# RMSNorm attention followed by a hard-swish MLP: moving the norms, joining the transposes, and issuing stores and output transposes later

## The chip, the cores and the metric

The kernel runs on one core of a Trainium2 chip. The metric is the device time of that core in microseconds (us). A run counts as slow when it is more than 1.5% above the fastest run of the same kernel; the kernel before was run again on the same chip beside every experiment. The kernel after was not: it is compared with an experiment through the ratios to the kernel before.

Names of the engines: PE is the matrix engine (PEld its weight loads), DVE the vector engine, ACT the scalar engine, POOL the general engine, SP the engine that here does nothing but issue DMA. Each executes its own list of instructions in order. An instruction that waits holds up everything behind it on its engine, related or not.

## The reference

Eight batches of twelve heads, 448 tokens, head size 64; then an MLP over the 3,584 tokens.

```python
def rmsnorm(x, g):
    rms = np.sqrt(np.mean(x * x, axis=-1, keepdims=True) + 1e-06)
    return x / rms * g
q_n, k_n = rmsnorm(q, g_q), rmsnorm(k, g_k)            # q, k, v: (8, 12, 448, 64)
scores = np.matmul(q_n, k_n.transpose(0, 1, 3, 2)) / np.sqrt(64)
attn = softmax(scores)                                 # over the keys
x = np.matmul(attn, v) -> (3584, 768)                  # heads side by side
h = x @ w_in                                           # (3584, 2048)
g = h * np.clip(h + 3.0, 0.0, 6.0) / 6.0
return g @ w_out                                       # (3584, 768), float32
```

## The kernel before

The kernel works on 48 pairs of heads, six pairs to a batch. Of a head's 448 tokens, 384 are "main" tokens (three blocks of 128); the remaining 64, the "rest tokens", are collected for all heads of two batches and normed and transposed together.

For a pair P: load q, k, v (SP); square (ACT for the first pairs, later POOL), sum (DVE), Ln and Exp (ACT) give the factor `rs`; POOL scales q and k into bf16 (`qks`) and copies v (`va`); SP issues crossbar transposes of `qks`; DVE multiplies the transposed keys with a mask and the gains (`kp`); PE makes seven score matmuls, ACT their exponentials, PE the products with v; DVE normalises into `xn`; SP transposes `xn` into `xT`. While batch b is in attention, PE also does h of batch b-1 (`h_part`, whose gate `gT` is made by DVE) and y of batch b-2 (`y_part`, copied from PSUM, the memory that PE writes its results to, by DVE into `y_sb` and stored by SP). The lists of SP and POOL stand in the order in which the program emits them. Cuts are marked; a comment starting with "note" is not in the kernel.

```python
def prep_pair(P):                       # note: norm and scaling of a pair in one go
    qk, vf = st.pop(("qk", P)), st.pop(("vf", P))
    sq = sq_pool.tile([128, 4 * NT * D], FP32, name="sq", tag="sq")
    qk_flat = qk[:].rearrange("p a h x -> p (a h x)")
    square(sq[:], qk_flat, P < 3)
    ssq = st_pool.tile([128, 4 * NT], FP32, name="ssq", tag="ssq")
    nc.vector.tensor_reduce(
        out=ssq[:], in_=sq[:].rearrange("p (n d) -> p n d", d=D), axis=AX_X, op=A_ADD)
    rs = rstd_of(ssq[:], 4 * NT)        # note: Ln, then Exp, both on ACT
    # ... cut: rs4 ...
    qks = qks_pool.tile([128, 2, NT, 2, D], BF16, name="qks")
    for i in range(2):
        nc.gpsimd.tensor_tensor(        # note: L162, waits on POOL for rs
            out=qks[:, i].rearrange("p t h d -> p h t d"),
            # ... cut ...
            op=A_MULT)
    # ... cut: POOL copies v into the ring va (L168) ...

def trans_rest(b):                      # note: rest tokens of batches b and b+1
    qks = st.pop(("qkrs", b))
    rT = rst_pool.tile([128, 2, NPAIR, 128], BF16, name="rT")
    nc.sync.dma_start_transpose(
        out=rT[:].rearrange("p a j c -> p (a j) c"), in_=qks[:].rearrange("p a h d -> p (a h d)"))
    for e in range(2):
        part = rT[:, :, :, e * 64:(e + 1) * 64]
        nc.vector.tensor_copy(out=qT_of(b + e)[:, :, SM:S], in_=part[:, 0])
        # ... cut: kbd, the masked rest keys, two multiplies on DVE ...

def trans_pair(P):
    b, j = divmod(P, NPAIR)
    qks = st.pop(("qks", P))
    nc.sync.dma_start_transpose(                                    # note: L237
        out=qT_of(b)[:, j, 0:SM].rearrange("p (t c) -> p t c", t=NT),
        in_=qks[:, 0].rearrange("p t h d -> p (t h d)"))
    kT = kT_pool.tile([128, SM], BF16, name="kT")
    nc.sync.dma_start_transpose(                                    # note: L241
        out=kT[:].rearrange("p (t c) -> p t c", t=NT),
        in_=qks[:, 1].rearrange("p t h d -> p (t h d)"))
    kp = kp_pool.tile([128, 2, SM], BF16, name="kp")
    for a in range(2):
        nc.vector.tensor_scalar_mul(kp[:, a, :], kT[:], gmask[:, a:a + 1])   # note: L246
    st["kp", P] = kp

def xtrans_rest(b, j0):                 # note: rest rows of x, three pairs
    xr = st["xr", b // 2]
    for j in range(j0, j0 + 3):
        nc.sync.dma_start_transpose(out=xT_of(b)[:, j, SM:SM + 128], in_=xr[:, j, :])

def y_part(G, i, nh, part):
    # ... cut: four matmuls per part, four parts ...
    if part == 3:
        y_sb = y_pool.tile([128, HALF], FP32, name="y_sb")
        nc.vector.tensor_copy(out=y_sb[:], in_=y_ps)                # note: L366
        cols = slice(nh * HALF, (nh + 1) * HALF)
        if i < NT:
            rows = out[G * S:G * S + SM, cols].rearrange("(p t) n -> t p n", t=NT)[i]
            nc.sync.dma_start(out=rows, in_=y_sb[:])                # note: L370
        # ... cut: rest rows, two stores (L374) ...

def att_items(P):
    b, j = divmod(P, NPAIR)
    n = P + 1
    items = [(0.0, lambda: load_step(P + 5)), (0.0, lambda: prep_step(P + 3)),
             (0.0, lambda: trans_step(P + 2))]
    sc = [(0.19, lambda u=u: score(n, u)) for u in range(NU)] if n < NP else []
    vs = [(0.3, lambda t=t: av(P, t)) for t in range(NT + 1)]
    items += merge(sc, vs)
    items.append((0.0, lambda: xtrans(P)))
    # ... cut: xtrans_rest after every third pair of odd batches ...
    return items

# ... cut ...
with tc.manual_schedule(engines={mybir.EngineType.SP, mybir.EngineType.Pool}):
    for P in range(5):
        load_step(P)
    for P in range(3):
        prep_step(P)
        if P < 2:
            trans_step(P)
    for u in range(NU):
        score(0, u)
    # ... cut: for each batch, the items of its six pairs merged with h and y items ...
```

## Time and profile before

| | before |
|---|---|
| median of three runs | 625.91 us (623.76 to 630.04) |
| profiled run: span, mean granted clock | 623.8 us, 0.901 |
| first exponential of pair 0, of pair 12, of pair 42 | 30.3, 161.4, 483.8 us |
| time of one batch in steady state (batches 4 to 6) | 64.7, 65.7, 66.1 us |

The "first exponential of pair n" is the (7n+1)th of the 336 score exponentials on ACT in the trace. It is a good clock of progress: batch b runs from the first exponential of pair 6b to that of pair 6b+6. I cut the span at pairs 0, 12 and 42 into start, front (pairs 0 to 11, while the MLP weights are loaded), steady part (pairs 12 to 41) and end.

The first lines of the profile page of the kernel before. Part 1 gives busy us, share of the span and number of instructions; part 2 shows the span in 40 slices, busy share in tenths, with the clock granted to PE; part 4 is the chain of work that ended last.

```profile
span 623.8 us, 9051 instructions
...
PE 461.5 (74%) x3344; PEld 257.1 (41%) x3344; DVE 253.5 (41%) x496; ACT 302.8 (49%) x582; POOL 212.8 (34%) x243
...
PE   0065234676579777969798989596988789789997
...
PEclk9997665799599998979799889898899999797999
...
issue 37%; POOL 24%; PE 16%; DMA 12%; SPq 6%; DVE 3%; POOLq 0%; ACT 0%; ACTq 0%
```

No engine is saturated. PE is the fullest with 74%, and the chain that ended last is made of PE for 16% only: it runs through POOL, DMA and "issue" (time in which an engine waited for nothing that the profile shows). In part 2 the slices of PE from the third to the eleventh (31 to 171 us) are on the whole the emptiest after the first two, and there the clock is lowest. So the kernel is bound by waits. Next, the view of windows for the three sections: us, then the busy time of each engine, PE's clock, DMA share, GB/s.

```profile
core 0: us, PE busy (x) PEld busy (x) DVE busy (x) ACT busy (x) POOL busy (x), PEclk, DMA share, GB/s
30.30:161.40 131.10, 70.60 (x540) 38.90 (x539) 44.89 (x94) 60.81 (x126) 56.21 (x63) 0.78 0.73 141
161.40:483.80 322.40, 268.45 (x1992) 149.04 (x1991) 151.89 (x294) 186.35 (x358) 136.51 (x146) 0.92 0.44 113
483.80:623.80 140.00, 121.87 (x812) 68.81 (x811) 48.95 (x94) 48.03 (x83) 9.23 (x11) 0.95 0.21 57
```

PE is busy for 71 of 131 us in the front, 268 of 322 in the steady part and 122 of 140 at the end. Which waits fill the rest shows the view of waits: what waited, for what, us in total, how many times, the longest.

```profile
POOL qks L162 <- ACT rs L128: 181.2, 44, 18.8
...
DVE kp L246 <- DMA kT<-qks: 130.6, 39, 11.4
PEld L261 <- DVE kp L246: 72.0, 28, 27.0
...
PE s_ps L261 <- DVE kp L246: 34.2, 21, 7.7
```

And the same view for the DMA queue of SP, i.e. what stood between SP and its next issue:

```profile
SPq L370 <- DVE y_sb L366: 127.8, 35, 7.8
...
SPq L374 <- DVE y_sb L366: 15.1, 5, 4.1
```

The waits of DVE, of PE and of SP form a ring. A few lines of the timeline at 212 us (start, duration, engine, line, operation; in brackets how long the engine sat idle before it, and for what) show one turn of it:

```profile
212.08 1.20 SPq L241 DMA_TRANSPOSE kT<-qks  x1
...
214.52 1.41 DVE L246 TENSOR_SCALAR kp<-kT,gmask 128x384 bf16<-128x384 bf16 x2 [2.44 <-DMA kT<-qks]
...
216.55 0.68 DVE L350 SCALAR_TENSOR_TENSOR gT_1502<-t_sb,h_ps 128x512 bf16<-128x512 f32 x1
217.14 0.55 DVE L366 COPY y_sb<-y_ps 128x384 f32<-128x384 f32 x1
217.28 0.81 PE L360 MATMUL y_ps<-w_out_sb,gT_819 128*128 128x384 bf16 x4 [1.16 <-DVE gT_1502 L350]
...
217.72 0.36 SPq L370 DMA_DIRECT2D out_dram<-y_sb  x1
```

SP issues the key transpose at 212.08, right before it is needed. DVE stands at the first instruction in its list that needs it, `kp`, and is idle for 2.44 us. Behind `kp` in DVE's list stand a gate and a y copy whose inputs are from earlier work; they run at 216.55 and 217.14. PE waits for that gate (217.28), which frees the PSUM buffer that h and y take in turn, and the store on SP can only go after the y copy (217.72). Only then does SP come to what stands behind the store: the next loads and transposes. SP waits for DVE; DVE waits for SP's transposes.

### The profile page before, as it was taken

What the parts mean: (1) busy time and instruction counts of PE and PEld (TensorE: products, weight loads), DVE (VectorE), ACT (ScalarE), POOL (GpSimd) and SP (SyncE); (2) the same over time, 40 slices, a digit from 0 to 9 for tenths busy, and PEclk for the clock granted to TensorE, in tenths of its full rate; (3) what the DMA queues carried; (4) which work ended last, traced back from release to release, by engine and by line L of the source; (5) the groups of instructions that cost most, each with busy time, mean ns of one, the idle gap of its engine ahead of it and who ended that gap; (6) DMA issues with size and microseconds to landing.
All of it is one profiled execution on the core that took longest, in us unless ns stands there. A gap on an engine that the chain in (4) does not pass through costs nothing.

```text
span 623.8 us, 9051 instructions
## 1 busy us (share of the span) xinstructions
PE 461.5 (74%) x3344; PEld 257.1 (41%) x3344; DVE 253.5 (41%) x496; ACT 302.8 (49%) x582; POOL 212.8 (34%) x243
## 2 busy tenths in 40 slices
PE   0065234676579777969798989596988789789997
PEld 0033122344145444535354546353544356454554
DVE  1342031264454544436346354353354543233331
ACT  2365223566466564646366655463656556332310
POOL 0745042455656332464135334552344220000000
PEclk9997665799599998979799889898899999797999
DMA  9498665994444245444353538343434332120012
GB/s 211 90 150 183 128 131 107 152 157 103 114 115 134 77 133 123 121 123 111 76 138 86 136 93 184 91 123 81 130 96 117 93 92 56 48 43 27 26 56 72
DMA packets 139660, 67.46 MB, mean 108 GB/s; under 512 B 92768, under 2 KB 138848, under 8 KB 139616
## 3 DMA queue, kind: packets, MB, share of 16 engines
q1 hardware_dynamic: 133184, 59.81, 39.2%
q0 software_dynamic: 2976, 6.29, 6.0%
q10 hardware_dynamic: 3456, 0.79, 0.8%
q8 instruction: 26, 0.43, 0.3%
q14 instruction: 18, 0.15, 0.1%
HBM read 45.61 MB, written 11.01 MB: 91 GB/s over the span
## 4 chain that ended last, share of the span: by engine, by line
issue 37%; POOL 24%; PE 16%; DMA 12%; SPq 6%; DVE 3%; POOLq 0%; ACT 0%; ACTq 0%
POOL sq L135 9%; PE y_ps L360 9%; POOL qks L162 8%; PE h_ps L343 6%; DMA kT<-qks 5%; SPq L332 3%; DMA qkr<-in_k_dram 2%; POOL vbd_89 L194 1%; POOL vbd_92 L194 1%; SPq L237 1%; PE s_ps L261 1%; SPq L325 1%; POOL sqr L135 1%; DMA qk<-in_k_dram 1%; POOL vbd_95 L194 1%
## 5 line engine op out<-in xcount | busy, mean ns | idle before, releaser
L262 ACT ACTIVATE eT<-s_ps,zero_c 128x448 bf16<-128x448 f32 x336 | 203.6, 635 | 158.7 <-PE s_ps L261 157.5
L261 PE MATMUL s_ps<-qT,kp 128*128 128x448 bf16 x288 | 112.3, 407 | 65.1 <-DVE kp L246 34.2
L162 POOL TENSOR_TENSOR qks<-qk,rs 128x384 bf16<-128x384 f32 x96 | 77.8, 832 | 189.7 <-ACT rs L128 181.2
L343 PEld LDWEIGHTS <-w_in_sb 128*128 128x128 bf16 x768 | 75.4, 102 | 109.5 <-issue 57.1
L348 ACT ACTIVATE t_sb<-h_ps,half_c 128x384 f32<-128x384 f32 (+1 forms) x128 | 80.6, 632 | 71.0 <-PE h_ps L343 70.5
L246 DVE TENSOR_SCALAR kp<-kT,gmask 128x384 bf16<-128x384 bf16 x96 | 43.0, 489 | 130.6 <-DMA kT<-qks 130.6
L270 PEld LDWEIGHTS <-eT 128*128 128x128 bf16 x1152 | 69.1, 104 | 58.8 <-DVE xn L289 18.7
L261 PEld LDWEIGHTS <-kp 128*128 128x128 bf16 x288 | 30.2, 107 | 112.4 <-DVE kp L246 72.0
L135 POOL TENSOR_TENSOR sq<-qk 128x768 f32<-128x768 f32 x45 | 66.2, 1471 | 0.2
L156 DVE TENSOR_REDUCE ssq<-sq 128x12 f32<-128x768 f32 x48 | 45.5, 948 | 30.9 <-POOL sq L135 22.8
L366 DVE COPY y_sb<-y_ps 128x384 f32<-128x384 f32 x56 | 30.8, 551 | 20.4 <-PE y_ps L360 20.2
L127 ACT ACTIVATE rs<-ssq,eps_c 128x12 f32<-128x12 f32 x48 | 14.6, 304 | 46.1 <-DVE ssq L156 46.0
L343 PE MATMUL h_ps<-xT_896,w_in_sb 128*128 128x512 bf16 x96 | 28.3, 395 | 8.4 <-DVE y_sb L366 5.0
L343 PE MATMUL h_ps<-xT_380,w_in_sb 128*128 128x384 bf16 x96 | 25.0, 378 | 12.5 <-DMA xT_380<-xn 10.2
L343 PE MATMUL h_ps<-xT_2374,w_in_sb 128*128 128x512 bf16 x96 | 28.2, 402 | 5.3 <-DMA xT_2374<-xr 4.2
L343 PE MATMUL h_ps<-xT_1599,w_in_sb 128*128 128x384 bf16 x96 | 22.3, 340 | 12.6 <-DVE y_sb L366 9.6
L343 PE MATMUL h_ps<-xT_3983,w_in_sb 128*128 128x512 bf16 x96 | 27.8, 397 | 4.3 <-DMA xT_3983<-xr 2.8
L343 PE MATMUL h_ps<-xT_5596,w_in_sb 128*128 128x512 bf16 x96 | 27.2, 406 | 3.1 <-DMA xT_5596<-xr 3.1
L360 PE MATMUL y_ps<-w_out_sb,gT_1502 128*128 128x384 bf16 x128 | 28.2, 343 | 0.3 <-DVE y_sb L366 0.3
L343 PE MATMUL h_ps<-xT_4817,w_in_sb 128*128 128x384 bf16 x96 | 21.9, 337 | 8.7 <-DVE y_sb L366 5.4
L360 PE MATMUL y_ps<-w_out_sb,gT_4720 128*128 128x384 bf16 x128 | 27.3, 338 | 1.1 <-DVE gT_5480 L350 1.0
L343 PE MATMUL h_ps<-xT_3208,w_in_sb 128*128 128x384 bf16 x96 | 22.1, 337 | 7.9 <-DVE y_sb L366 6.6
(81 smaller groups left out, 636.3 us busy)
## 6 DMA issues: line engine op xcount, KB each, us to landing
qk<-in_q_dram SPq DMA_DIRECT2D x48, 192.0 KB, 2.7
qk<-in_k_dram SPq DMA_DIRECT2D x48, 192.0 KB, 2.7
vf<-in_v_dram SPq DMA_DIRECT2D x48, 192.0 KB, 3.3
out_dram<-y_sb SPq DMA_DIRECT2D x48, 192.0 KB, 1.9
w_in_sb<-in_moe_w_in_dram POOLq DMA_DIRECT2D x6, 512.0 KB, 8.3
w_out_sb<-in_moe_w_out_dram POOLq DMA_DIRECT2D x4, 768.0 KB, 7.6
vr<-in_v_dram SPq DMA_DIRECT2D x16, 96.0 KB, 3.4
out_dram<-y_sb SPq DMA_DIRECT2D x16, 96.0 KB, 2.2
```

The lines of the kernel that those rows point to most:

```text
L135: nc.gpsimd.tensor_tensor(out=out, in0=x, in1=x, op=A_MULT)
L156: nc.vector.tensor_reduce(out=ssq[:], in_=sq[:].rearrange("p (n d) -> p n d", d=D), axis=AX_X, op=A_ADD)
L162: nc.gpsimd.tensor_tensor(out=qks[:, i].rearrange("p t h d -> p h t d"), in0=qk[:, i].rearrange("p h (t d) -> p h t d", d=D), in1=rs4[:, i ...
L194: nc.gpsimd.tensor_scalar(vbd[:, :, a * E1:a * E1 + D], vr[:], mask[:, a:a + 1], None, A_MULT)
L246: nc.vector.tensor_scalar_mul(kp[:, a, :], kT[:], gmask[:, a:a + 1])
L261: nc.tensor.matmul(out=ps[:], lhsT=lhsT, rhs=st["qT", b][:, j, :], start=True, stop=True)
L262: nc.scalar.activation(out=st["e", P][:, u, :], in_=ps[:], func=EXP, bias=zero_c[:], scale=1.0)
L270: nc.tensor.matmul(out=dst[:, a * E1:(a + 1) * E1], lhsT=eT[:, u, c0:c0 + 128], rhs=va[:, a, t, :], start=(first and a == 0 and t == 0), s ...
L343: nc.tensor.matmul(out=h_ps[:, 0:n], lhsT=w_in_sb[:, kt, f * 128:(f + 1) * 128], rhs=st["xT", G][:, kt, :], start=(kt == 0), stop=(kt == N ...
L348: nc.scalar.activation(out=t_sb[:, 0:n], in_=h_ps[:, 0:n], func=RELU, bias=half_c[:], scale=1.0 / 6.0)
L360: nc.tensor.matmul(out=y_ps, lhsT=gT[:, f, i * 128:(i + 1) * 128], rhs=w_out_sb[:, f, nh * HALF:(nh + 1) * HALF], start=(f == 0), stop=(f ...
L366: nc.vector.tensor_copy(out=y_sb[:], in_=y_ps)
```

## The change

Its intent, in the words that came with it: norms one pair ahead of the scaling; one crossbar transpose for keys and queries of a pair; stores and output transposes issued later; rest tokens loaded first. In parts:

- **norm**: square, sum, Ln and Exp of pair P+4 are done in the step before the scaling of that pair, so POOL's scaling finds `rs` ready. Loads go to P+6.
- **joined transposes**: one transpose of six blocks of 128x128 (keys, then queries) in place of two of three; one of three for the rest rows of x in place of three of one. It costs a DVE copy of 64 rest columns per pair and one of `xrT` per half.
- **store**: the store of a y group is emitted in the middle of the next group. **late xT**: the transpose of `xn` is emitted near the end of the next pair's step.
- **start**: three pairs loaded before the first norms instead of five, keys before queries, rest loads split over SP and ACT, rest scaling of batch 0 on DVE.

The core of the diff; cuts are pool sizes (`st_pool` 4 to 8, `y_pool` 3 to 4, four `kq` buffers in place of three `kT` and three `qT`), the weight of the value products when lists are merged (0.3 to 0.25), squares on ACT for four pairs instead of three, the split of `prep_rest` alike to that of `prep_pair`, and engine choices of the first loads.

```diff
-    def prep_pair(P):
-        qk, vf = st.pop(("qk", P)), st.pop(("vf", P))
+    def norm_pair(P):
+        qk = st["qk", P]
         sq = sq_pool.tile([128, 4 * NT * D], FP32, name="sq", tag="sq")
 # ... cut ...
-        rs = rstd_of(ssq[:], 4 * NT)
+        st["rs", P] = rstd_of(ssq[:], 4 * NT)
+
+    def prep_pair(P):
+        qk, vf, rs = st.pop(("qk", P)), st.pop(("vf", P)), st.pop(("rs", P))
 # ... cut ...
     def trans_pair(P):
-        b, j = divmod(P, NPAIR)
         qks = st.pop(("qks", P))
+        kq = kq_pool.tile([128, SM + S], BF16, name="kq")
         nc.sync.dma_start_transpose(
-            out=qT_of(b)[:, j, 0:SM].rearrange("p (t c) -> p t c", t=NT),
-            in_=qks[:, 0].rearrange("p t h d -> p (t h d)"))
-        kT = kT_pool.tile([128, SM], BF16, name="kT")
-        nc.sync.dma_start_transpose(
-            out=kT[:].rearrange("p (t c) -> p t c", t=NT),
-            in_=qks[:, 1].rearrange("p t h d -> p (t h d)"))
+            out=kq[:, 0:2 * SM].rearrange("p (t c) -> p t c", c=128),
+            in_=qks[:].rearrange("p a t h d -> p (a t h d)"))
+        st["kq", P] = kq
+
+    def pad_pair(P):
+        b, j = divmod(P, NPAIR)
+        kq = st.pop(("kq", P))
+        e = (b % 2) * 64
+        nc.vector.tensor_copy(out=kq[:, 2 * SM:], in_=st["rT", b // 2][:, 1, j, e:e + 64])
         kp = kp_pool.tile([128, 2, SM], BF16, name="kp")
         for a in range(2):
-            nc.vector.tensor_scalar_mul(kp[:, a, :], kT[:], gmask[:, a:a + 1])
+            nc.vector.tensor_scalar_mul(kp[:, a, :], kq[:, 0:SM], gmask[:, a:a + 1])
+        st["qT", P] = kq[:, SM:]
         st["kp", P] = kp
 # ... cut ...
     def xtrans_rest(b, j0):
         xr = st["xr", b // 2]
-        for j in range(j0, j0 + 3):
-            nc.sync.dma_start_transpose(out=xT_of(b)[:, j, SM:SM + 128], in_=xr[:, j, :])
+        xrT = xr_pool.tile([128, 3, 128], BF16, name="xrT")
+        nc.sync.dma_start_transpose(
+            out=xrT[:], in_=xr[:, j0:j0 + 3, :].rearrange("p j c -> p (j c)"))
+        nc.vector.tensor_copy(out=xT_of(b)[:, j0:j0 + 3, SM:SM + 128], in_=xrT[:])
 # ... cut ...
     def y_part(G, i, nh, part):
+        if part == 2:
+            flush_stores()
 # ... cut ...
+            stores.append(lambda: y_store(G, i, nh, y_sb))
 # ... cut ...
-        items = [(0.0, lambda: load_step(P + 5)), (0.0, lambda: prep_step(P + 3)),
-                 (0.0, lambda: trans_step(P + 2))]
+        items = [(0.0, lambda: load_step(P + 6)), (0.0, lambda: norm_step(P + 4)),
+                 (0.0, lambda: trans_step(P + 2)), (0.0, lambda: prep_step(P + 3))]
 # ... cut ...
-        items.append((0.0, lambda: xtrans(P)))
-        if b % 2 == 1 and j % 3 == 2:
-            items.append((0.0, lambda: xtrans_rest(b, j - 2)))
+        items.insert(len(items) - 6, (0.0, flush_late))
+
+        def done():
+            late.append(lambda: xtrans(P))
+            if b % 2 == 1 and j % 3 == 2:
+                late.append(lambda: xtrans_rest(b, j - 2))
+            if j == NPAIR - 1:
+                flush_late()
+        items.append((0.0, done))
 # ... cut ...
-        for P in range(5):
+        for P in range(3):
             load_step(P)
-        for P in range(3):
+        norm_step(0)
+        norm_step(1)
+        for P in range(2):
             prep_step(P)
-            if P < 2:
-                trans_step(P)
+            trans_step(P)
+            load_step(P + 3)
+            norm_step(P + 2)
+        prep_step(2)
+        load_step(5)
```

## The prediction

> **What bounds the kernel now.** Nothing is saturated: PE is busy 461.5 of 623.8 us, ACT 302.8, DVE 253.5, POOL 212.8 (page, part 1). Warm and fed, PE needs about 440 us (estimate from trace durations: 336 scores at 0.19, 192 groups of seven small value products at 0.45, 768 + 896 MLP matmuls at 0.19 and 0.163 us). The kernel is bound by waits in in-order queues:
> 1. Start: first score at 29.7 us (timeline); the rest tokens' keys are loaded last, issuing them holds ACT until 12.65 us, and the score needs the rest transpose.
> 2. 30 to 161 us (pairs 0 to 11): PE half busy. POOL's scaling waits 181.2 us in all for the ACT root of its own pair (view of waits), so transposes go out late and meet weight loads (one key transpose: issued 61.0, used 73.5 us). DMA is about 75% busy (windows).
> 3. Batches 4 to 6: 65 us each, PE busy 56 (windows). SP waits 127.8 us for y_sb before stores, transposes queued behind; DVE waits 130.6 us for kT before kp, gate and y_sb copies queued behind; PE waits 106 us for kp.
>
> **What the change does.**
> - Norm of pair P+4 ahead of scaling of P+3: POOL no longer waits for reduce, Ln, Exp (4 us per pair); this reaches PE only through the transposes.
> - 48 pair transposes and 16 of the rest of x fewer, 1.2 us of SP issue each: 77 us of SP. Added on DVE: 48 copies of 64 columns, 8 of xrT, about 10 us, which has room.
> - Stores wait for the next y group, xT transposes for the end of the next pair: their data are then ready and block nothing. kp should be ready a step early.
> - Start: three pairs loaded instead of five, keys of the rest second, 2.75 instead of 3.9 MB before the first score; qkrs scaled on DVE.
> - Matmuls, exps and bytes unchanged.
>
> **On the critical path.** Start: -10 us. 30 to 161: -28 (weights took 37 us of 16-engine DMA time, a pair about 4.4, so 100 us is near the floor). Batches 2 and 3: -13. Batches 4 to 6: -5 each of a possible 8, since h still waits at each batch start for the last xT. Batch 7 and end: -4. Sum -70: **555 us, 530 to 590** (8 in 10). Faster by over 2% 0.95, within 2% 0.04, slower 0.01.
>
> The Trainium skill ("TensorE: Matmul & The Clock Gate", the HAM clock gate) says PE falls to half clock after an idle window of about 3.4 us. This trace agrees: scores take 581 ns around the stalls at 75 to 125 us, 349 later. Fewer gaps should raise the mean clock from 0.90 to about 0.94, part of the gain above.
>
> **What would show it.** First score at 19 us. First exp of pair 12 at 120 to 135 us (161 before). POOL's wait for ACT below 40 us, SP's for y_sb below 15, DVE's for pair transposes below 50, PE's for kp below 35. Batches 4 to 6 at 59 us. PE share 80% or more.
>
> **What would make it wrong.** If early DMA is already at its limit, the front yields only the start. If one transpose of six blocks lands much later than the 2.4 us of three, or behind six pairs of loads, kp stays late. If steady waits merely become h waiting for xT (xr now passes through DVE) or PSUM waiting for y_sb, batches stay at 65 us: about 590. If PE takes all the room, 530.

## The result, and the profile after

| | before | after |
|---|---|---|
| median | 625.62 us (four runs) | 532.87 us (526.60 to 535.94, four runs) |
| ratio of fast runs, 95% interval | | 0.8475 (0.8384 to 0.8566) |
| profiled run: span, clock | 623.8 us, 0.901 | 530.6 us, 0.945 |
| start (to the first exponential) | 30.3 us | 24.1 us |
| front, pairs 0 to 11 | 131.1 us | 94.7 us |
| steady part, pairs 12 to 41 | 322.4 us | 290.8 us |
| end, pair 42 on | 140.0 us | 121.0 us |
| batches 4, 5, 6 | 64.7, 65.7, 66.1 us | 57.0, 62.6, 58.0 us |

The ratios are made from fast runs; they are not quite the ratios of the medians quoted. The change is 15% faster, more than predicted, inside the range. The profiled spans differ by 93.2 us: start 6.2, front 36.5, batches 2 and 3 together 12.5, batches 4 to 6 together 18.9, batch 7 and the end 19.1.

The same lines of the page of the kernel after:

```profile
span 530.6 us, 8957 instructions
...
PE 433.2 (82%) x3316; PEld 251.9 (47%) x3344; DVE 262.6 (49%) x546; ACT 299.4 (56%) x583; POOL 210.7 (40%) x244
...
PE   0245559957899987799799988589798999999996
...
PEclk9985768979999999899899999899999999999999
...
PE 45%; DMA 20%; issue 11%; DVE 10%; POOL 8%; SPq 4%; ACT 1%; POOLq 0%; DVEq 0%
```

PE now makes 45% of the chain that ended last, where it made 16%. One trap: the page counts 3,316 matmuls and 3,344 weight loads. 28 records of h matmuls are missing from this trace, 24 in the steady part and 4 at the end; at 0.28 us each (busy time of the recorded ones of that shape over their number, as their records overlap) PE was busy some 8 us longer than the page says, about 441 us. Still 20 us less than before for the same matmuls, because the clock was higher. Idle times of PE below are corrected in this way, for this trace and for the experiments that lack the same 28 records.

The windows of the sections, with the columns of before:

```profile
24.10:118.80 94.70, 62.10 (x490) 35.11 (x488) 45.30 (x97) 59.08 (x126) 60.06 (x66) 0.77 1.04 205
118.80:409.60 290.80, 255.63 (x2018) 149.37 (x2042) 158.08 (x332) 185.27 (x359) 130.90 (x140) 0.98 0.56 128
409.60:530.60 121.00, 114.90 (x807) 67.08 (x811) 47.32 (x95) 46.65 (x81) 6.11 (x8) 1.00 0.20 55
```

The front's DMA share rose from 0.73 to 1.04, which suggests that the front is now held by what it loads; experiment 11 tests it. (The share counts the times of packets, and reaches 1.13 in the first half of this front: 1 is not its ceiling.) In the steady part PE is idle for about 28 us instead of 54, at a clock of 0.98 instead of 0.92. At the end PE is idle for about 5 us instead of 18, and works at full clock, 116 us (corrected) instead of 122.

The waits that answer to those of before:

```profile
DVE kp L250 <- DMA kq<-qks: 82.4, 30, 10.6
POOL va L171 <- PE r_ps L275: 80.4, 17, 7.1
POOL va L171 <- PE r_ps L278: 64.6, 10, 9.7
...
PEld L266 <- DVE kp L250: 27.0, 6, 18.1
...
POOL qks L164 <- ACT rs L128: 23.1, 8, 4.9
...
PE s_ps L266 <- DVE kp L250: 7.1, 2, 6.7
```

POOL's wait for its own norm fell from 181.2 to 23.1 us. POOL is not quicker for it: it now waits for PE to release the ring of v copies, 145 us in these two lines, and that is spare time, since it comes from being ahead. PE's wait for `kp` (matmuls and weight loads added, though the two overlap in part) fell from 106.2 to 34.1 us, of which 18.1 is the start. DVE still waits 82.4 us for the pair transposes. And SP:

```profile
SPq L388 <- DVE y_sb L375: 85.8, 24, 6.3
SPq L330 <- DVE y_sb L375: 60.9, 11, 7.3
...
SPq L392 <- DVE y_sb L375: 11.8, 4, 4.4
```

SP waits for `y_sb` for 158.5 us in these three lines, against 142.9 in the two of before. The wait that the change set out to remove is still there; what changed is what stands behind it. I measured how long before the first exponential of its pair DVE began `kp` (median of pairs 12 and later), and call this its lead: 1.9 us before, 11.1 us after, about a whole step of a pair.

A turn of the ring after the change, in the timeline:

```profile
265.29 1.22 SPq L238 DMA_TRANSPOSE kq<-qks  x1
...
269.05 0.55 DVE L250 TENSOR_SCALAR kp<-kq,gmask 128x384 bf16<-128x384 bf16 x2 [2.37 <-DMA kq<-qks]
...
270.21 0.68 DVE L357 SCALAR_TENSOR_TENSOR gT<-t_sb,h_ps 128x512 bf16<-128x512 f32 x1
...
270.80 0.55 DVE L375 COPY y_sb<-y_ps 128x384 f32<-128x384 f32 x1
```

DVE still comes to `kp` before its transpose, issued 3.8 us earlier, has landed, stands idle for 2.37 us, and makes the gate and the y copy after it. The difference to before is that PE doesn't need this `kp` yet.

The start of the kernel after, in its timeline:

```profile
20.61 2.76 DVE L229 TENSOR_SCALAR kbd<-rT,gmask 128x384 bf16<-128x384 bf16 x4 [1.16 <-DMA rT<-qkrs]
...
23.51 1.79 PE L266 MATMUL s_ps<-kq,kp 128*128 128x448 bf16 x4 [23.51 <-DVE kq L247]
```

The rest transpose has landed at 20.6 us, where the first score could follow, but DVE first makes four `kbd` multiplies (2.76 us) that stand ahead of the pad copy `kq<-rT` that the score needs.

### The profile page after: what moved, and what is told of

It reads as the page before. It is cut to its first block, busy times and chain, and to the rows that moved or that the text cites. A ratio compares the mean times of both kernels' runs of the same rounds, so it can differ in the third digit from the quotient of the medians.

```text
span 530.6 us, 8957 instructions
## 1 busy us (share of the span) xinstructions
PE 433.2 (82%) x3316; PEld 251.9 (47%) x3344; DVE 262.6 (49%) x546; ACT 299.4 (56%) x583; POOL 210.7 (40%) x244
## 4 chain that ended last, share of the span: by engine, by line
PE 45%; DMA 20%; issue 11%; DVE 10%; POOL 8%; SPq 4%; ACT 1%; POOLq 0%; DVEq 0%
PE y_ps L369 17%; PE h_ps L350 17%; DMA kq<-qks 10%; PE s_ps L266 6%; DMA xT<-xn 3%; POOL sq L135 3%; PE x_ps L275 3%; DVE kp L250 3%; DMA qk<-in_q_dram 2%; POOL qks L164 2%; DVE gT L357 2%; DMA vf<-in_v_dram 2%; SPq L142 1%; DVE ssq L155 1%; DVE y_sb L375 1%
## 5 line engine op out<-in xcount | busy, mean ns | idle before, releaser
L350 PE MATMUL h_ps<-xT,w_in_sb 128*128 128x384 bf16 (+1 forms) x740 | 185.8, 357 | 44.5 <-DVE y_sb L375 16.0
L369 PE MATMUL y_ps<-w_out_sb,gT 128*128 128x384 bf16 x896 | 180.3, 329 | 7.5 <-DVE gT L357 7.4
L266 PE MATMUL s_ps<-kq,kp 128*128 128x448 bf16 x288 | 107.8, 386 | 33.1 <-DVE kq L247 24.8
L369 PEld LDWEIGHTS <-gT 128*128 128x128 bf16 x896 | 85.1, 98 | 66.8 <-issue 13.9
L357 DVE SCALAR_TENSOR_TENSOR gT<-t_sb,h_ps 128x384 bf16<-128x384 f32 (+1 forms) x128 | 78.8, 617 | 63.1 <-ACT t_sb L355 62.3
L171 POOL CAST va<-vf 128x384 bf16<-128x384 f32 x48 | 24.5, 510 | 182.7 <-PE r_ps L275 80.4
L164 POOL TENSOR_TENSOR qks<-qk,rs 128x384 bf16<-128x384 f32 x96 | 77.8, 831 | 32.2 <-ACT rs L128 23.1
L250 DVE TENSOR_SCALAR kp<-kq,gmask 128x384 bf16<-128x384 bf16 x96 | 43.9, 490 | 82.7 <-DMA kq<-qks 82.4
L275 PE MATMUL x_ps<-va,eT 128*128 128x65 bf16 x864 | 59.1, 200 | 7.0 <-DVE xn L294 6.6
L278 PE MATMUL x_ps<-vbd,eT 128*128 128x130 bf16 x144 | 32.5, 225 | 0.5 <-ACT eT L267 0.3
L294 DVE TENSOR_TENSOR xn<-x_ps,rd 128x384 bf16<-128x384 f32 x48 | 26.6, 555 | 1.2
L275 PE MATMUL r_ps<-va,eT 128*128 128x65 bf16 x288 | 24.1, 201 | 0.0
```

Source lines behind the costliest of these rows:

```text
L164: nc.gpsimd.tensor_tensor(out=qks[:, i].rearrange("p t h d -> p h t d"), in0=qk[:, i].rearrange("p h (t d) -> p h t d", d=D), in1=rs4[:, i ...
L250: nc.vector.tensor_scalar_mul(kp[:, a, :], kq[:, 0:SM], gmask[:, a:a + 1])
L266: nc.tensor.matmul(out=ps[:], lhsT=lhsT, rhs=st["qT", P], start=True, stop=True)
L275: nc.tensor.matmul(out=dst[:, a * E1:(a + 1) * E1], lhsT=eT[:, u, c0:c0 + 128], rhs=va[:, a, t, :], start=(first and a == 0 and t == 0), s ...
L350: nc.tensor.matmul(out=h_ps[:, 0:n], lhsT=w_in_sb[:, kt, f * 128:(f + 1) * 128], rhs=st["xT", G][:, kt, :], start=(kt == 0), stop=(kt == N ...
L357: nc.vector.scalar_tensor_tensor(out=st["gT", G][:, f, :], in0=t_sb[:, 0:n], scalar=1.0, in1=h_ps[:, 0:n], op0=A_MIN, op1=A_MULT)
```

## The experiments

All twelve gave correct results. Those named u_ are the kernel after with one part undone; those named b_ are the kernel before with one part done. I give ratios with their intervals, and all of them differ clearly from 1 but that of b_norm. What counts below is the distance from 0.8475 (0.8384 to 0.8566), the whole change: the intervals of u_store, u_late, u_start and w_out_later overlap with it. Sections and first exponentials are those of the profiled run.

### 1. u_norm: undo the norm ahead

```diff
-        items = [(0.0, lambda: load_step(P + 6)), (0.0, lambda: norm_step(P + 4)),
-                 (0.0, lambda: trans_step(P + 2)), (0.0, lambda: prep_step(P + 3))]
+        items = [(0.0, lambda: load_step(P + 6)), (0.0, lambda: trans_step(P + 2)),
+                 (0.0, lambda: norm_step(P + 3) if P else None), (0.0, lambda: prep_step(P + 3))]
```

> The changed kernel with one part undone: in the loop the norm of a pair is taken just before its own scaling again (pair P+3), not one pair ahead. Theory A (POOL held by the root of its own pair was what made the front slow): POOL's wait for ACT comes back to over 120 us in all, first exp of pair 12 moves from 119 to 130 us or later, total 545 to 555 us. Rival B (scaling three pairs ahead has slack enough, the front is at the limit of the DMA engines whatever POOL does): POOL's wait comes back, but pair 12 stays within 4 us of 119 and the total within 1% of 533.

Measured: median 544.64 us, ratio 0.8789 (0.8717 to 0.8862) against the 0.8475 of the whole change. Pair 12 starts at 139.7 us. POOL's wait for `rs` is back:

```profile
POOL qks L164 <- ACT rs L128: 131.7, 41, 13.7
```

The front takes 116.1 us in place of 94.7; the steady part is 281.6, if anything shorter. So the norm ahead is worth about 20 us by the ratios (0.8789 less 0.8475, times 625), 12 by the profiled runs and the medians, and all of it in the front. It is not a share of the front's gain of 36.5 that can be added to others: undoing the xT part alone (experiment 3) lengthens the front as much. This is A, just under its range for the total.

### 2. u_store: store at once

```diff
-            stores.append(lambda: y_store(G, i, nh, y_sb))
+            y_store(G, i, nh, y_sb)
```

> Undone alone: each output store is issued right after its copy again. Theory A (stores waiting for y_sb block the transposes behind them on SP): SP's wait for y_sb rises well above the 158 us of the changed kernel, DVE waits for kq in the steady batches again, batches of the steady part get 2 to 4 us longer each, total 540 to 550. Rival B (SP waits for y_sb nearly as long after the change, so those waits are spare time of a queue that is ahead): total within 1% of 533.

Measured: median 535.64 us, ratio 0.8633 (0.8539 to 0.8726). The profiled run was a slow one (545.67), so its sections are not read. The interval overlaps that of the whole change: the loss is about 10 us by the ratios, 3 by the medians, and not clear of noise. That is B, within 1% of 533.

### 3. u_late: transpose of xn at the end of its own step

```diff
         def done():
-            late.append(lambda: xtrans(P))
+            xtrans(P)
             if b % 2 == 1 and j % 3 == 2:
-                late.append(lambda: xtrans_rest(b, j - 2))
-            if j == NPAIR - 1:
-                flush_late()
+                xtrans_rest(b, j - 2)
```

> Undone alone: output transposes of a pair are issued at the end of its own step again. Theory A: SP sits at the transpose until the pair's normalisation is done, loads and key transposes of the next step start later, total 538 to 548. Rival B: the transposes of a pair are needed a step later and there is slack, and xT even lands earlier, total within 1% of 533.

Measured: median 535.48 us, ratio 0.8627 (0.8544 to 0.8710). The interval overlaps that of the whole change, and the total is B's. It hides two opposite movements: the front takes 115.8 us (94.7), the steady part 271.8 (290.8). The edit also moved instructions in DVE's list: `kp` now stands later in it, and in the steady part DVE waits 38.4 us for the pair transposes in place of 53.7. I can't separate this from the effect on SP by this run. It gave the idea of experiment 9.

### 4. u_store_late: both undone

The two edits above together.

> Both undone: stores and output transposes at once. Theory A: SP stands at these two waits as it did before the change, DVE waits for kq again by some 40 us more than the changed kernel in the steady batches, total 550 to 565, more than the sum of the two single losses if each covers for the other. Rival B: total within 1.5% of 533, and the steady gain must come from the joined transposes.

Measured: median 573.12 us, ratio 0.9254 (0.9180 to 0.9329), above even A's range. The two alone cost at most about 10 us each, together 49 (0.9254 less 0.8475, times 625; 40 by the medians). So each covers for the other, as I read it: if either the store or the xT transpose is out of the way, SP gets through. With neither, SP's wait for `y_sb` at the stores is 157.6 us in its largest line, the lead of `kp` is only 3.4 us instead of 11.1, and PE waits 93.4 us for it (60.2 + 33.2), nearly the 106.2 of before. This is the ring again.

```profile
SPq L388 <- DVE y_sb L375: 157.6, 36, 7.9
```

### 5. u_trans: split the transposes

```diff
-        nc.sync.dma_start_transpose(
-            out=kq[:, 0:2 * SM].rearrange("p (t c) -> p t c", c=128),
-            in_=qks[:].rearrange("p a t h d -> p (a t h d)"))
+        for i in (1, 0):
+            nc.sync.dma_start_transpose(
+                out=kq[:, i * SM:(i + 1) * SM].rearrange("p (t c) -> p t c", c=128),
+                in_=qks[:, i].rearrange("p t h d -> p (t h d)"))
 # ... cut: and xr straight into xT, three transposes of one block, no copy on DVE ...
```

> Undone alone: two transposes of three blocks for a pair's keys and queries again, and one per block for the rest of x, straight into xT. Theory A (64 issues of 1.2 us less on SP matter): SP is busy 77 us more, in the front kq lands later behind the weight loads, total 540 to 550. Rival B (SP has over 150 us of waits in the changed kernel, so issue time is free; bytes are the same): total within 1% of 533, and xT of the odd batches a little earlier without its copy.

Measured: median 578.63 us, ratio 0.9239 (0.9161 to 0.9316): 48 us, much more than expected, and the largest single part of the change. It costs in every section: the front takes 102.8 us (94.7), the steady part 316.6 (290.8), the end 128.3 (121.0). It keeps the order of instructions of ACT, that of DVE but for the eight copies of `xrT`, which go, and that of PE but for 36 of 6,688 places, so this is a matter of SP and DMA. The trace has 172 transposes on SP for 221.6 us against 108 for 148.3 us. What one costs SP, from the view of one tile (min, median, max of the duration in ns): first of u_trans, then of the kernel after.

```profile
L239 SPq DMA_TRANSPOSE kq<-qks x96: 1177/1246/2744, 14.2 to 476.7; - x96
```

```profile
L238 SPq DMA_TRANSPOSE kq<-qks x48: 1215/1217/8024, 14.8 to 438.7; - x48
```

A six-block transpose takes 1.22 us of SP, a three-block one 1.25. (In the kernel before, the medians of the two are 1.20 each.) Between three and six blocks the issue time hardly depends on the size, so joining two gives one issue back. The data don't come later: the median from issue to landing is 3.6 us for six blocks and 3.2 for three, and the second of two is issued a transpose later. The wait in the ring that grows is DVE's, from 82.4 us to

```profile
DVE kp L251 <- DMA kq<-qks: 122.5, 36, 10.8
```

### 6. u_start: the old start

```diff
-        for P in range(3):
+        for P in range(5):
             load_step(P)
 # ... cut: norm_step(0), norm_step(1), loop head ...
-            load_step(P + 3)
 # ... cut: rest loads on ACT, rest scaling on POOL, gains loaded by ACT, as before ...
```

> Undone alone: the start, with five pairs loaded first, rest keys and queries on the ACT queue, gains on the ACT queue, rest scaled on POOL. Theory A: first score from 23.5 back to about 29 us, and the whole kernel later by that, 538 to 540 us. Rival B (the front is DMA-limited: the same bytes must pass before pair 12): first score at 29 us but pair 12 within 2 us of 119, total within 0.5% of 533.

Measured: four runs at 534.26, 539.96, 551.13 and 555.60 us, the last two slow; ratio of the fast ones 0.8603 (0.8528 to 0.8679). The first exponential comes at 33.0 us in place of 24.1, but the front is then 91.5 in place of 94.7, and the profiled run ends at 532.5, 1.9 us after the other. The new start is worth 9 us at the first exponential, and by the runs between 2 us (profiled runs) and 8 us (ratios), intervals overlapping, so nothing is shown for the total. Pair 12 comes at 124.5 us, later than B said; neither theory is decided.

### 7. b_norm: the norm ahead alone

In the kernel before, `prep_pair` split as in the change and

```diff
-        items = [(0.0, lambda: load_step(P + 5)), (0.0, lambda: prep_step(P + 3)),
+        items = [(0.0, lambda: load_step(P + 5)), (0.0, lambda: norm_step(P + 4)), (0.0, lambda: prep_step(P + 3)),
                  (0.0, lambda: trans_step(P + 2))]
```

> The kernel before with the norm ahead as the only change. Theory A (POOL is a main cause): POOL's wait for ACT falls from 181 to below 60 us and the total to 585 to 605. Rival B (transposes stay blocked on SP by stores and output transposes, so POOL being early frees nothing): POOL's wait falls, but the total stays within 1.5% of 626.

Measured: median 626.65 us, ratio 1.0037 (0.9945 to 1.0130), with two of the four runs (630.30 and 634.54) slow: nothing. The front is shorter (112.8 us for 131.1), the steady part longer (337.6 for 322.4). POOL's wait for `rs` fell from 181.2 to 21.7 us, and turned into these, in the view of waits of b_norm:

```profile
POOL sq L135 <- DMA qk<-in_k_dram: 242.5, 39, 11.0
DVE ssq L156 <- POOL sq L135: 116.2, 32, 6.4
```

The square of pair P+4 now waits for the load of P+4, which is in SP's list behind the stores and transposes; DVE then stands at `ssq`, a wait of 116.2 us that was 22.8 before. POOL was waiting for the ring in another place. That a norm ahead pays only once the loads come early enough is my reading: the norm alone with loads at P+6 was not run.

### 8. b_store_late: later stores and xT transposes alone

In the kernel before, the `stores` and `late` lists of the change, nothing else.

> The kernel before with later stores and later output transposes as the only change. Theory A (SP blocked by these is the main cause in the steady batches): batches 4 to 6 from 65 to below 61 us, total 590 to 605. Rival B (POOL's wait for the root keeps the transposes late whatever SP does): total within 1.5% of 626. If neither this nor the norm alone gives much, each of the two holds the same chain and only both together release it.

Measured: median 600.09 us, ratio 0.9613 (0.9569 to 0.9657), 24 us. Batches 4 to 6 take 61.3, 64.8 and 63.0 us: the total is in A's range, the batches are not. The lead of `kp` is 11.2 us, as in the whole change: it comes from this part. But the time gained is half of what the same part is worth inside the whole change (49 us, experiment 4).

### 9. kp_later: a new edit, DVE's wait moved behind ready work

In the kernel after, DVE still waits 82.4 us at `kp` though it begins `kp` 11 us before its pair's first exponential, and gates and y copies stand behind it. So: from pair 14 on, emit the pad copy and `kp` later in the step, and keep the scheduler from placing them ahead of the last gate or y copy.

```diff
-            nc.vector.scalar_tensor_tensor(
+            st["g"] = nc.vector.scalar_tensor_tensor(
 # ... cut: likewise for the copy into y_sb, and in trans_step ...
-        pad_pair(P)
+    def pad_after(P):
+        if P < 14:
+            return pad_pair(P)
+        with tc.issue_after(st["g"].ins):
+            pad_pair(P)
 # ... cut ...
         items.insert(len(items) - 6, (0.0, flush_late))
+        if P + 2 < NP:
+            items.insert(len(items) - 6, (0.0, lambda: pad_after(P + 2)))
```

> The changed kernel; from pair 14 on kp and its pad copy are held on DVE behind the gate or y copy that was recorded just before, which puts them about one pair later in DVE's order. PE's order stays exactly the same. Theory C (in the steady part the loss sits on DVE: kp stands in its queue before its transpose has landed, and the gate and y copies wait behind it, so PE stalls at h and y): DVE's wait for kq between pairs 12 and 42 falls from 54 to below 15 us, PE's idle there from 35 to below 22 us, total 512 to 523. Rival D (PE's remaining stalls at h come from y_sb and the gate themselves, DVE waits only when it has nothing else to do): DVE's wait for kq falls but PE idles as before, total within 1% of 533.

Measured: median 505.83 us (504.38 to 507.63), ratio 0.8096 (0.8050 to 0.8143): faster than both kernels, 4.5% below the change by the ratios, and more than C expected. PE's list is the same in all 6,688 places, ACT's in 580 of 583. Part 1 of its page; then the steady part in its windows (columns as above); then a line of its view of waits, and one of the same view for SP's queue:

```profile
PE 431.3 (86%) x3344; PEld 252.5 (50%) x3344; DVE 253.5 (50%) x546; ACT 299.6 (60%) x583; POOL 210.4 (42%) x244
```

```profile
117.60:383.00 265.40, 252.31 (x2043) 148.99 (x2044) 150.41 (x330) 184.86 (x359) 128.76 (x138) 0.99 0.61 140
```

```profile
DVE kp L250 <- DMA kq<-qks: 25.1, 10, 10.5
```

```profile
SPq L330 <- DVE y_sb L375: 12.5, 3, 6.2
```

DVE's wait for the pair transposes is 25.1 us in place of 82.4; in the steady part alone 1.7 in place of 53.7. SP's wait for `y_sb` at the xT transposes is 12.5 in place of 60.9, though no instruction of SP was changed. The steady part takes 265.4 us in place of 290.8, with 13 us of PE idle in place of about 28 and 252 us busy in place of about 262 for the same matmuls. What became of the wait, in the timeline:

```profile
258.99 1.21 SPq L238 DMA_TRANSPOSE kq<-qks  x1
...
270.93 0.69 DVE L357 SCALAR_TENSOR_TENSOR gT<-t_sb,h_ps 128x512 bf16<-128x512 f32 x1 [2.38 <-ACT t_sb L355]
...
271.62 0.54 DVE L250 TENSOR_SCALAR kp<-kq,gmask 128x384 bf16<-128x384 bf16 x2
```

Each transpose has its `kp`, in the same order; counted along the two lists, the `kp` at 271.62 belongs to the transpose issued at 258.99, and the gate at 270.93 now stands ahead of it. The data landed long ago, so `kp` doesn't wait. Its lead is 4.2 us (median) instead of 11.1, and that is enough.

### 10. u_trans_kp_later: split transposes under the held kp

The edits of 5 and 9 together.

> The same hold on kp, with the transposes split again (two per pair, three for each half of the rest), which alone cost about 45 us. Theory C (splitting made the kp that stands too early on DVE wait longer, that is how it cost so much): most of the loss goes away, total 520 to 540. Rival E (64 more issues on SP cost by themselves, as SP's time between its waits for y_sb is in the loop that sets the pace): total stays 560 or more.

Measured: one fast run, the profiled one, at 531.01 us; the others, 540.52 to 546.79, count as slow, so there is no ratio. Against the profiled run of kp_later (spans 529.2 and 502.6) the split costs 26.6 us: 7.8 in the front, 15.8 in the steady part, 2.3 at the end. Without the hold the profiled runs of 5 and of the change differ by 40.8. So, by this one fast run, about a third of the cost of the split ran through DVE's wait at `kp`, and the rest did not. The totals, 531 to 547, are in C's range or just above it and none is E's, but only because the hold gains 27 us with joined transposes too, which neither had allowed for: most of the loss did not go away. Why this kernel's times scatter more than the others, I don't know.

### 11. w_out_later: the second weights four pairs later

```diff
-        if NPAIR <= P < NPAIR + 4:
-            load_w_out(4 * (P - NPAIR))
+        if NPAIR + 4 <= P < NPAIR + 8:
+            load_w_out(4 * (P - NPAIR - 4))
```

> The changed kernel with the four loads of w_out issued four pairs later (with the scaling of pairs 10 to 13 instead of 6 to 9); nothing else. Theory F (after the change the front, pairs 0 to 11, is held by the DMA engines, which are full in the trace from 24 to 119 us; w_out is about 20 us of their time and is needed only from pair 12): the time from the first exp of pair 0 to that of pair 12 falls from 95 to 85 us or less, total 522 to 528. Rival G (the front waits for POOL, SP and DVE in turn and DMA is only busy beside it): the front stays within 3 us of 95 and the total within 0.7% of 533, or longer if y then waits for w_out.

Measured: median 536.42 us, ratio 0.8583 (0.8530 to 0.8635), no gain. Batch 0 falls from 49.4 to 42.9 us, batch 1 rises from 45.3 to 58.3. F is right that the weights cost time where they are loaded; G is right on the total, but not on the front, which is 101.3 us: the cost moves with them, and is larger in the later place. (It is not y that waits: the last of these loads is issued at 107.3 us, the first y matmul comes at 132.0 and waits for a gate.) So what limits the front after the change stays open.

### 12. b_joined: the joined transposes alone

In the kernel before: `trans_pair`, `pad_pair`, `xtrans_rest` and the order keys before queries of the change; norm and scaling together, stores and xT transposes at once, loads at P+5, the old start.

> The kernel before with the joined transposes as the only change (one of six blocks for a pair, one of three for each half of the rest of x, with their small copies; keys before queries). Norm, stores, output transposes and start as before. Theory H (SP's issue time is part of the loop SP to transposes to DVE to y_sb to SP, so 64 issues of 1.2 us less shorten every step): total 590 to 608, pairs 12 to 42 from 322 to below 305 us, with DVE still waiting for the transposes. Rival I (as with the norm alone: one link made shorter while stores and output transposes hold SP gives nothing): total within 1.5% of 624.

Measured: median 580.58 us, ratio 0.9328 (0.9252 to 0.9405), 42 us, better than expected. The steady part falls from 322.4 to 301.1 us, the front from 131.1 to 117.5, and DVE's wait for the transposes from 130.6 to 107.1 us. H is right, and the total better than its range: fewer issues on SP pay by themselves, with stores and norms where they were. (The `kq` ring of four came with the edit; u_trans, which keeps that ring, costs about as much.)

```profile
DVE kp L250 <- DMA kq<-qks: 107.1, 39, 6.1
```

### What the twelve say together

| part | done alone, in before | undone alone, in after |
|---|---|---|
| norm ahead | +2 us (1.0037) | 20 us (0.8789) |
| later stores and xT transposes | -24 us (0.9613) | 49 us (0.9254) |
| joined transposes | -42 us (0.9328) | 48 us (0.9239) |
| start | not run | 8 us (0.8603) |

Each is the difference of the ratio from 1, or from 0.8475, times 625 us. The sizes are uncertain by up to 7 us: by the mean times of the fast runs the right column reads 13, 42, 46 and 6, since the kernel before ran faster beside the first two (619.9 us in the mean of its fast runs, against 626.3 beside the change). Done alone, the three bring 64 us of the 95 that the whole change brings; undone alone, the four cost 125 (108 by the times). Parts that act on separate stretches would give the same sum in both columns. These share one ring, which is the reading that fits: each part is worth more when the others have opened it.

## Why the prediction was right or wrong

**Right: what bounds the kernel, and the way to the gain.** "The kernel is bound by waits in in-order queues": every experiment that moved the time did so with the same matmuls. PE's share of at least 80% (82%) and the mean clock of about 0.94 (0.945) came in. The mechanism cited from the Trainium skill, "TensorE: Matmul & The Clock Gate", Part 1: The HAM clock gate (half clock after an idle window of about 3.4 us), is in agreement with the traces in its two clocks and its period: the clock records of the trace before have only the values 1 and 0.5, in stretches of 3.41 us and multiples of it, and score matmuls take 581 ns at the slowest and 353 at the median in the trace after. It is not in agreement on the idle window: 12 of the 15 falls to 0.5 before the end of the trace before came right after 3.41 us in which PE was busy for part of the time, up to 1.63 us; in the 6.8 us before the fall at 428.4 us, PE's longest single gap was 1.0 us. So in these traces short waits add up to a fall, without one long gap. Half clock took 52.0 us of the steady part before, 13.7 after and 6.8 in kp_later. So an idle gap that is taken away can pay twice.

**Right: batches 2 and 3, and 4 to 6.** "Batches 2 and 3: -13" measured 12.5; "Batches 4 to 6: -5 each" measured 18.9 in all, a mean of 59.2 us where 59 was said.

**Right in kind, too small: "30 to 161: -28".** It measured 36.5; pair 12 came at 118.8, just under the 120 to 135 said. POOL's wait for ACT fell to 23.1 (below 40 was said), PE's for `kp` to 34.1 (below 35). Undoing the norm gives 21 us of the front back, and the DMA share there is 1.04. I had put the floor of these 131 us "near" 100; it is 91.5 or less (u_start).

**Too large: "Start: -10".** It measured 6.2: the first score came at 23.5, not 19. The step that failed is that I looked for the landing of the rest transpose, and not at DVE's list after it: four multiplies of 2.76 us in all stand ahead of the copy that the score needs. That is 2.8 of the 4.5 us missed; the rest transpose itself landed only at 20.6.

**Mis-sized: "Batch 7 and end: -4".** It measured 19.1, and this is the largest single error. I had judged this stretch by its last 81 us, where PE was 91% busy (73.5 us), and left out that batch 7 still runs the loop of the other batches: from the first exponential of pair 42 to that of pair 47 it fell from 59.3 to 46.4 us, and the rest from 80.8 to 74.6. Split otherwise, about 13 us of it is PE's idle time (18.1 to about 5) and 6 its busy time (121.9 to about 116) at a clock of 1.00 instead of 0.95. The sum predicted was 70 and the gain of the profiled runs is 93.2; the errors of its terms are +15.1 here, +8.5 in the front, +3.9 in batches 4 to 6, -0.5 in batches 2 and 3 and -3.8 at the start.

**Wrong: "Stores wait for the next y group, xT transposes for the end of the next pair: their data are then ready and block nothing".** SP's wait for `y_sb` was to fall below 15 us and is 158.5. The data are not ready, because SP runs ahead of PE and DVE: however late in the list the store stands, SP gets there early and stands. What the later place does is to let the pair transposes of the next pairs go before the wait. The lead of `kp`, 1.9 us before and 11.1 after, and 11.2 with this part alone (experiment 8), shows this. So "kp should be ready a step early" was right, but not for the reason given: in this part the prediction was lucky.

**Wrong: DVE's wait for pair transposes below 50 us.** It is 82.4. I reasoned from when PE needs `kp`, but DVE waits when its list comes to `kp`, which is early. The Trainium skill says in "TensorE: Matmul & The Clock Gate", Architectural detail, that ACT and DVE are strictly first in, first out; the traces agree, as gate and y copy with ready inputs run only after `kp`. Experiment 9 shows the cost: with the instructions of DVE in another order, and nothing else but 3 places of ACT's list, 27 us (532.87 less 505.83; 24 by the ratios).

**What the joined transposes gained.** I had counted "77 us of SP" and given no share of the sum to it. The trace shows 70 us less (218.7 to 148.3). Experiments 5 and 12 show 42 to 48 us of time from it. The skill's page "DMA: Bandwidth & Descriptors", Rules for kernel authors, says to coalesce many small transfers, and that under 64 KB one mostly pays overhead. That agrees in direction; but the transposes of pairs joined here were already of 98 KB each (128 x 384 in bf16), those of xr of 33 KB, and one, three and six blocks alike cost SP 1.2 us in the median.

**What stays open.** How the cost of the split transposes divides between those of pairs and those of xr; how much of u_late's shorter steady part is DVE's order, and why its front is 21 us longer; how the interaction of about 31 us (95 less 64, start included) divides; and whether the start gains 2 to 3 us if the `kbd` multiplies stand behind the pad copy, which I did not run.

## What to carry to other kernels

Before moving work, draw the ring: which engine's in-order list waits for which, and what ready work stands behind each wait. An instruction is best placed in its engine's list where its input has landed, neither where its output is first needed nor as early as it can be emitted; kp_later gained 4.5% by letting the multiplies of `kp` stand behind a gate or a copy that was ready. And expect parts that open the same ring to be worth little alone and much together: test them undone as well as done.

## What the Trainium skill lacked or had wrong

- "DMA: Bandwidth & Descriptors" has no time for transposes from SBUF to SBUF of a few blocks (it has cycles for 8,192 tiles, and bandwidths). Here a transpose takes SP 1.19 to 1.25 us for three blocks of 128x128 and 1.22 for six; from issue to landing the median is 2.3 to 3.3 us for three and 3.6 for six.
- Its rule to coalesce is put in bytes, with 64 KB as the mark. What joining saved here was issues, 1.2 us of SP each at any of the sizes: with transposes of 98 KB joined in twos and some of 33 KB in threes, 6.7% (b_joined).
- Its rule to issue a DMA early and wait late (Rules for kernel authors) is right, but doesn't say that on an in-order engine "late" means late in that engine's list, behind other ready work. Issuing at the same place and only waiting later gave 27 us (kp_later, "DVE kp" waiting 25.1 us for the transposes in place of 82.4).
- "TensorE: Matmul & The Clock Gate" (Part 1: The HAM clock gate) has the clock fall after an idle window, but doesn't say how much work a window can hold and still count as idle. Here the clock fell after windows of 3.41 us with up to 1.63 us of PE busy (12 of 15 falls in the trace before). What such falls cost in all: PE was busy 461.5 us in the kernel before and 431.3 in kp_later for the same 3,344 matmuls, a difference of 4.8% of the span of before.
